# Chunked delta-rule attention with a phase mixer: accumulating products and a tile's transposes issued as several operations each, under a new order, new banks and new engine choices

## The chip, the cores and the metric

The kernel runs on one core of one Trainium2 chip. The metric is the time of one execution in microseconds on the device. Five engines work from queues of their own, each in the order written: TensorE (PE, with its weight loads as PEld), VectorE (DVE), ScalarE (ACT), GpSimd (POOL) and SyncE (SP), which issues most DMA transfers. Inputs and output are float32 in HBM; products run in bfloat16.

## The reference

Four batches of eight heads with 768 steps and 40 channels per head go through a recurrence with a state of 40 x 40 per head. Its output, as 768 x 320 per batch, goes through a mixer with rotated phases.

```python
for t in range(S):
    y[:, :, t] = einsum('bhd,bhde->bhe', rt, state)
    Sa = einsum('bhde,bhe->bhd', state, at)
    state = state * wt[:, :, None, :] - einsum('bhd,bhe->bhde', Sa, bt) \
            + einsum('bhd,bhe->bhde', vt, kt)
# x: (B, S, H*D)
theta = x @ w_theta
zr, zi = x * cos(theta), x * sin(theta)
y = einsum('ts,bsd->btd', w_tok_r, zr) + einsum('ts,bsd->btd', w_tok_i, zi)
u = x + y
out = u + maximum(u @ w_ch, 0)
```

## The kernel before

**Tiles.** A tile is 128 steps of one batch with all heads, 128 x 320. There are 24, six for each batch, numbered i. For each, `prep` takes the logarithm of w (`ln`), sums it along time with a triangular product (`cs`), takes exponentials (`exp` and others) and scales k, b and a with them. Features of 64 rows per head (40 and padding) are turned with PE transposes into `feat`. For tiles 0 to 5 (`TURNED`) raw k, b and a are instead loaded in another layout, two tiles at a time, cast by POOL into `turning` (a view of a z buffer, so the profile shows it as z; `ck`, `cb`, `ca`), turned by PE while still unscaled (`tkbr` for k and b, `tar` for a), and scaled by DVE on the way out of PSUM (`mk`, `mb`, `ma`, L625 and L628). Their exponentials sit in single buffers, `exi` and `exw`.

**Scores and recurrence.** `scores` (L668) makes four products per tile of 128 x 128 per head: psi, phi and the two halves of lam. Each is masked to a triangle on the way from PSUM to SBUF: by DVE with a mask (L676), or by ACT as a plain copy (L678) and then POOL's select (L680). `recurrence` makes x0 = psi v + a state (L712 and L707 in one accumulation), nx, then nu with phi, and the new state gt from k v and b nu (L745). `readout` makes y from the state (L836) and both halves of lam (L842); DVE's `ex` product gives x.

**Mixer.** `theta` turns x for two tiles (`xt`), `sines` multiplies by w_theta and takes cosine and sine on ACT, and z = x cos, x sin is made by POOL or DVE (`product`, L493 and L492). `mix_row` makes a row of the token mixing from twelve products of 320 columns (L896), the largest part of PE's work; it can begin only when the six tiles of a batch are through the recurrence. `channels` then does the product with w_ch and stores. The weights come by POOL's own DMA issues, which also convert to bfloat16: w_theta and w_ch by L935, blocks of w_tok into `wrow` by L946. A copy within SBUF on POOL or ACT (`ws0`, `ws1`) repeats parts of w_theta and w_ch in a second place, since later products read them on other rows.

**Order.** Every step is first recorded as an operation (`Op`) by `Plan.add`, with its engine and with what it reads and writes. `ORDER` lists the numbers of all operations; each engine executes its own in that order. `HOMES` gives the PSUM banks, in the order in which operations open them. `PICK` lists the operations that take their other form, on another engine or as whole transposes (`turn_whole`, 128 x 128, L424) instead of two of 64 rows (`turn`, L419). `WARM` puts idle products (L994) ahead of some operations. An operation is indivisible in this order:

```python
out = [self.ops[n] for n in ORDER]
```

Ahead of the first operation each engine prepares masks and zeroed pads; on POOL the last of this is `sign_col` (L389).

Of the kernel before, what the change touches and what calls it, by code (L numbers as in the profile page):

```python
# [20 lines left out]
LATE = 12  # L21
ORDER = [
# [218 lines left out]
def mm(n):  # L241
    return max(n / 2.4 + 2.5, 25.0)
# [7 lines left out]
def kernel(  # L250
# [252 lines left out]
    def prep(i):  # L503
# [12 lines left out]
        def cs():  # L516
# [7 lines left out]
            if late:  # L524
                return
# [517 lines left out]
```

## Time and profile before

| What | Value |
|---|---|
| Median of 3 runs | 194.38 us (193.88 to 195.51) |
| Span of the profiled execution | 191.6 us |
| Timed runs above the span | 2.3 to 3.9 us, at the median 2.8 |
| Own time of the profiled execution | not recorded apart from its span |
| PE, DVE busy | 179.6, 165.7 us |
| ACT, POOL busy | 157.9, 136.9 us |
| Mean granted TensorE clock | 0.991 |

The span runs from the first to the last instruction on the core. Busy time of PE is a union of overlapping products, so a busy PE need not be at its peak. Rows of a group give the line, engine, operation, tiles and shape, then the busy time in us, the mean duration of one in ns, and after the second bar the idle time of the engine just ahead of them with what ended it. Tile names leave the buffer number out.

### The profile page before, as it was taken

How to read it: one execution, taken by the hardware profiler on the slowest of the kernel's cores; microseconds unless marked ns; L12 is line 12 of the kernel's file. 1: busy time of each engine (PE TensorE's matmuls, PEld its weight loads, DVE VectorE, ACT ScalarE, POOL GpSimd, SP SyncE). 2: the span in 40 equal slices, each digit the busy share in tenths (PEclk: the TensorE clock that was granted, in tenths of full speed). 3: DMA queues.
4: the chain of work that ended last, by engine and by line, in shares of the span. 5: the costliest groups of instructions: out<-in, count | busy, mean ns of one | idle time of the engine just before them, and what ended most of it. 6: DMA issues, size and time to landing. Idle time of an engine off the chain costs nothing.

```text
span 191.6 us, 9477 instructions
## 1 busy us (share of the span) xinstructions
PE 179.6 (94%) x4223; PEld 142.0 (74%) x4223; DVE 165.7 (86%) x268; ACT 157.9 (82%) x288; POOL 136.9 (71%) x162
## 2 busy tenths in 40 slices
PE   7679799999898999999999999999999999999992
PEld 7567587787687877788777787868877877876751
DVE  7599899998899998999889978998999998886552
ACT  3499999999999999989999979799999769883010
POOL 5584595496799789989989396694999983643200
PEclk9969999999999999999999999999999999999999
DMA  5999799989889999999997999999927011001131
GB/s 131 321 310 323 182 244 205 178 150 160 164 137 211 187 187 174 201 215 193 197 207 171 154 191 210 179 169 238 217 38 168 12 37 38 3 3 68 68 140 68
DMA packets 110312, 30.90 MB, mean 161 GB/s; under 512 B 98624, under 2 KB 110272, under 8 KB 110272
## 3 DMA queue, kind: packets, MB, share of 16 engines
q1 hardware_dynamic: 107840, 27.53, 66.6%
q0 software_dynamic: 2432, 2.77, 9.1%
q8 instruction: 33, 0.54, 1.1%
q14 instruction: 7, 0.06, 0.1%
HBM read 29.13 MB, written 3.93 MB: 173 GB/s over the span
## 4 chain that ended last, share of the span: by engine, by line
PE 74%; DVE 13%; ACT 7%; DMA 2%; issue 1%; SPq 1%; POOL 0%; ACTq 0%
PE ps L896 22%; PE ps L419 12%; PE ps L668 10%; PE ps L810 6%; DVE lam L676 4%; PE ps L842 4%; PE ps L424 3%; DMA raw_a<-in_a_dram 2%; PE ps L745 2%; PE ps L816 2%; PE ps L724 2%; PE ps L712 2%; PE ps L836 2%; PE ps L707 2%; PE ps L518 2%; DVE feat L625 2%
## 5 line engine op out<-in xcount | busy, mean ns | idle before, releaser
L676 DVE TENSOR_TENSOR lam<-ps,mask_p 128x1024 bf16<-128x1024 f32 x39 | 47.1, 1219 | 3.6 <-PE ps L668 3.3
L896 PE MATMUL ps<-z,wtok 128*128 128x320 bf16 x288 | 48.2, 299 | 0.0
L493 POOL TENSOR_TENSOR z<-cs,xp 128x640 bf16<-128x640 f32 x21 | 29.2, 1403 | 4.5 <-ACT cs L874 4.4
L896 PEld LDWEIGHTS <-wtok 128*128 128x128 bf16 x288 | 24.3, 97 | 9.1 <-issue 0.2
L493 POOL TENSOR_TENSOR kb<-raw_kb,ex 128x640 bf16<-128x640 f32 x18 | 25.8, 1433 | 2.0 <-ACT nx L718 1.3
L676 DVE TENSOR_TENSOR psi<-ps,mask_p 128x1024 bf16<-128x1024 f32 x19 | 23.1, 1219 | 1.1 <-PE ps L668 1.0
L668 PEld LDWEIGHTS <-feat 64*128 64x128 bf16 x576 | 18.0, 95 | 6.6 <-issue 4.4
L668 PE MATMUL ps<-feat 64*128 64x128 bf16 x384 | 18.4, 221 | 1.9 <-ACT exi L611 0.9
L676 DVE TENSOR_TENSOR phi<-ps,mask_n 128x1024 bf16<-128x1024 f32 x13 | 15.9, 1220 | 1.6 <-PE ps L668 1.6
L680 POOL TENSOR_SCALAR_AFFINE_SELECT phi<-phi 128x1024 bf16<-128x1024 bf16 x11 | 12.0, 1092 | 7.0 <-ACT phi L678 7.0
L842 PE MATMUL ps<-kb,lam 128*128 128x40 bf16 x384 | 15.5, 180 | 0.2 <-DVE lam L676 0.2
L452 ACT COPY feat<-ps 128x1024 f32<-128x1024 f32 (+1 forms) x14 | 14.0, 998 | 0.6 <-PE ps L419 0.5
L842 PEld LDWEIGHTS <-lam 128*128 128x128 bf16 x384 | 13.8, 96 | 0.8 <-issue 0.3
L642 ACT COPY rT<-ps 128x512 bf16<-128x512 bf16 x24 | 13.3, 600 | 0.3 <-PE ps L419 0.2
L509 ACT ACTIVATE lw<-raw_w 128x320 bf16<-128x320 f32 x24 | 11.4, 483 | 2.4 <-DMA raw_w<-in_w_dram 2.3
L680 POOL TENSOR_SCALAR_AFFINE_SELECT lam<-lam 128x1024 bf16<-128x1024 bf16 x9 | 9.8, 1090 | 4.9 <-ACT lam L678 4.9
L901 DVE TENSOR_TENSOR up<-ps,xp 128x320 bf16<-128x320 f32 x22 | 10.6, 487 | 2.8 <-PE ps L896 2.5
L493 POOL TENSOR_TENSOR ah<-raw_a,ex 128x320 bf16<-128x320 f32 x15 | 12.1, 806 | 0.7 <-ACT ex L544 0.4
L452 ACT COPY uT<-ps 128x320 f32<-128x320 f32 (+1 forms) x9 | 3.6, 404 | 10.8 <-PE ps L419 5.4
L678 ACT ACTIVATE phi<-ps 128x1024 bf16<-128x1024 f32 x11 | 11.4, 1033 | 1.0 <-PE ps L668 1.0
L836 PE MATMUL ps<-gd,rT 128*128 128x80 bf16 x80 | 12.2, 197 | 0.0
L728 ACT ACTIVATE nu<-ps 128x320 bf16<-128x320 f32 x24 | 10.8, 450 | 1.5 <-PE ps L724 1.2
(165 smaller groups left out, 538.4 us busy)
## 6 DMA issues: line engine op xcount, KB each, us to landing
raw_w<-in_w_dram SPq DMA_DIRECT2D x24, 160.0 KB, 4.7
raw_r<-in_r_dram SPq DMA_DIRECT2D x12, 320.0 KB, 5.0
out_dram<-oo SPq DMA_DIRECT2D x11, 320.0 KB, 3.1
raw_a<-in_a_dram SPq DMA_DIRECT2D x18, 160.0 KB, 4.5
raw_kb<-in_k_dram SPq DMA_DIRECT2D x18, 160.0 KB, 4.2
raw_kb<-in_b_dram SPq DMA_DIRECT2D x18, 160.0 KB, 4.4
raw_v<-in_v_dram SPq DMA_DIRECT2D x16, 160.0 KB, 5.0
raw_v<-in_v_dram SPq DMA_DIRECT2D x4, 320.0 KB, 5.7
```

What stands on the lines that cost most here:

```text
L419: nc.tensor.transpose(out=dst[:, c, n * 64:n * 64 + 64], in_=block[rows(c)], identity=ident[rows(c), rows(c)])
L452: nc.scalar.copy(out=to, in_=source)
L493: pool = ("POOL", lambda: nc.gpsimd.tensor_tensor(out=dst, in0=in0, in1=in1, op=ALU.mult))
L509: add("ACT", "ln", i, lambda: nc.scalar.activation(out=heads(lw)[:, :, 0:D], in_=raw_w[s4], func=AF.Ln), 473, [("raw_w", s4)], [("lw", s2) ...
L642: add("ACT", "e" + nm, i + x, lambda x=x, dst=dst: nc.scalar.copy(out=dst.rearrange("p g (t q) -> p g t q", q=8), in_=ps(pr).bitcast(BF16) ...
L668: nc.tensor.matmul(t[:, q, g, :], lhsT=lhs[rows(q), g, :], rhs=rhs[rows(q), g, :], start=True, stop=True)
L676: add("DVE", kindm, i, lambda: nc.vector.tensor_tensor(out=flat, in0=whole(), in1=mask.to_broadcast([128, 2 * G, 128]), op=ALU.mult), 1217 ...
L680: add(None, "sel", i, None, 0, dkeys, dkeys, alts=(("POOL", lambda: nc.gpsimd.affine_select(out=flat, in_=flat, pattern=[[0, 2 * G], [1, 1 ...
L810: nc.tensor.matmul(ps(pk)[:, c, 0:DM], lhsT=lhs[:, 3 * c + kt, :], rhs=wt[:, 3 * c + kt, :], start=kt == 0, stop=False, skip_group_check=True)
L836: nc.tensor.matmul(t[:, g * 80:g * 80 + 80], lhsT=rT[:, g, :], rhs=gd[:, 2 * g:2 * g + 2, :], start=True, stop=False, skip_group_check=True)
L842: nc.tensor.matmul(t[:, h * D:h * D + D], lhsT=lam[:, n, p, g, :], rhs=kb[:, n, h, 0:D], start=first and n == 0, stop=n == 1, skip_group_c ...
L896: nc.tensor.matmul(ps(pk)[:, 0:DM], lhsT=wtok[t % NCH][:, c, s, :], rhs=z[:, c, s], start=s == 0 and c == 0, stop=s == NT - 1 and c == 1)
```

## The change

Operations are split where they add into one bank:

- `x0` becomes `x0` (psi v) and `x0s` (the carried state); `y` becomes `yv`, `ys` (state) and `y`; `gt` becomes `gtk` (k v) and `gt` (b nu).
- `cs` loses its last product to `csx`, for tiles before 12.
- The transposes of a tile's features, `tt`, become `tta` (k and b), `ttb` (a) and `ttc` (v), each waiting for its own source alone.

Within a bank the products now mark only the first of them as one that begins the sum. `ORDER` grows from 1390 to 1520 numbers, `PICK` from 134 to 165; `HOMES` has as many entries, with other values. `WARM` places the idle products of the start ahead of other operations, in equal numbers. `TURNED` stays at six tiles. A path for `SIDES` is new, but that set is empty.

Core of the diff:

```diff
+SIDES = frozenset()
 ORDER = [
-    0, 3, 13, 14, 15, 16, 4, 21, 17, 5, 18, 19, 6, 20, 23, 22, 25, 59, 62, 26, 24, 64, 67, 63,
...
+    168, 52, 54, 0, 3, 17, 4, 18, 13, 14, 15, 22, 20, 5, 6, 1, 19, 21, 23, 24, 16, 26, 27, 60,
...
-WARM = {14: (38, 0), 19: (10, 3), 20: (2, 3), 62: (4, 3)}
+WARM = {14: (38, 0), 20: (10, 4), 21: (2, 6), 64: (4, 0)}
...
+        if groups:
+            m = 0
+            for c, (count, keys) in enumerate(groups):
+                add("PE", kind + "abc"[c], i, lambda m=m, count=count: turn(
+                    ps(p).bitcast(BF16), blocks[m:m + count], m), reads=keys, writes=[p],
+                    at=at, new=(p, 2) if c == 0 else None, **quad_cost(4 * count))
+                m += count
...
+        add("PE", "cs", i, cs, mm(328) + 4 * 25, [("lw", s2)], [pk],
+            new=(pk, 1 if late else 2), tail=tail(2))
+        if not late:
+            add("PE", "csx", i, earlier, mm(328), [("lw", s2)], [pk], tail=tail(328))
...
         def x0():
             t = ps(pk)
+            for h in range(H):
+                nc.tensor.matmul(t[:, h * D:h * D + D], lhsT=psi[:, h % 2, h // 2, :],
+                                 rhs=vb[:, h, 0:D], start=h == 0, stop=True,
+                                 skip_group_check=True)
+
+        def carried():
+            t = ps(pk)
             for g in range(G):
...
+                nc.tensor.matmul(t[:, g * 80:g * 80 + 80], lhsT=feat[:, 8 + g, :],
+                                 rhs=gt_old[:, g, :, 0:D], start=False, stop=True,
+                                 skip_group_check=True)
+        add("PE", "x0", i, x0, 8 * 25, [("psi", i % NSC), ("v", i % NRV)], [pk], new=(pk, 1),
+            tail=tail(40))
+        if not first:
+            add("PE", "x0s", i, carried, 4 * mm(80), [("fa", st), ("gt", (i + 1) % 2)], [pk],
+                tail=tail(80))
...
+            add("PE", "gtk", i, lambda: gains(kb[:, 0], vb, True),
+                4 * mm(80) + (mm(320) if join else 0), [("kb", i % NKB), ("v", i % NRV)] +
                 ([("gt", (i + 1) % 2)] if join else []), [gk], new=(gk, 1), tail=tail(80))
+            add("PE", "gt", i, lambda: gains(kb[:, 1], nu, False), 4 * mm(80),
+                [("kb", i % NKB), ("nu", s2)], [gk], tail=tail(80))
...
+        add("PE", "yv", i, lambda: y(0), 8 * 25, [("lam", s2, 0), ("kb", i % NKB)], [pk],
+            new=(pk, 1), tail=tail(40))
+        if not first:
+            add("PE", "ys", i, carried, 4 * mm(80), [("rT", i % 6), ("gd", (i + 1) % 2)], [pk],
+                tail=tail(80))
+        add("PE", "y", i, lambda: y(1), 8 * 25, [("lam", s2, 1), ("kb", i % NKB)], [pk],
+            tail=tail(40))
```

What it moves shows best in the engines' own orders. **POOL at the start**, from the end of its preparation. In these rows raw_kb and raw_a are the loads of k, b and a for tiles 0 and 1, z the buffer that `turning` looks into, and wth the weights of w_theta. Before:

```order
L389 AFFINE_SELECT sign_col_197<-sign_col_197 64x1 x2
L499 CAST z_1_190<-raw_kb_0_71 128x16x40
L499 CAST z_1_190<-raw_kb_1_72 128x16x40
L499 CAST z_1_190<-raw_a_0_68 128x16x40
L499 CAST o_0_130<-raw_v_0_75 128x16x40
L935 DMA wth_233<-in_moe_w_theta_dram 64x320
L499 CAST r_0_132<-raw_r_0_78 128x16x40
```

Now:

```order
L401 AFFINE_SELECT sign_col_197<-sign_col_197 64x1 x2
L991 DMA wrow_1_208<-in_moe_w_tok_r_dram 128x768
L980 DMA wth_233<-in_moe_w_theta_dram 128x2x320
L521 COPY wth_233<-wth_233 64x640
L521 CAST z_1_190<-raw_kb_0_71 128x16x40
L521 CAST z_1_190<-raw_kb_1_72 128x16x40
L521 CAST z_1_190<-raw_a_0_68 128x16x40
L521 CAST r_0_132<-raw_r_0_78 128x16x40
```

Two DMA issues and the copy that repeats a part of wth have moved ahead of the casts; the copy reads what the second of these DMAs writes.

**PE at x0 of tile 10**, with its neighbours (psi and v of that tile, gt the state carried in; products of 320 columns are token mixing, or the sums of a later tile's ln w). Before, the state's products stood between those with psi:

```order
L896 MATMUL ps_0_235<-z_0_189,wtok_0_201 128x320
L707 LDWEIGHTS feat_1_151
L707 MATMUL ps_1_236<-gt_1_137,feat_1_151 128x80
L712 LDWEIGHTS psi_0_158
L712 MATMUL ps_1_236<-v_2_140,psi_0_158 128x40
```

Now:

```order
L730 MATMUL ps_3_238<-v_2_140,psi_0_158 128x40
L941 LDWEIGHTS wtok_1_202
L941 MATMUL ps_1_236<-z_0_189,wtok_1_202 128x320
...
L540 MATMUL ps_1_236<-lw_0_82,ntri_inc_88 128x328
...
L737 LDWEIGHTS feat_1_151
L737 MATMUL ps_3_238<-gt_1_137,feat_1_151 128x80
```

The eight products with psi run first, a piece of the mixing and the sums of another tile stand between, and the four with the state come last into the same bank.

More of the change, by code (lines that the diff above doesn't have):

```diff
@@ L21 @@
 LATE = 12
+SIDES = frozenset()
+SLOT = ((0, 3, 1, 4, 2), (2, 0, 3, 1, 4))
 ORDER = [
[81 rows of a table removed]
-HOMES = [
[13 rows of a table removed]
-PICK = [
[8 rows of a table removed]
-WARM = {14: (38, 0), 19: (10, 3), 20: (2, 3), 62: (4, 3)}
[89 rows of a table added]
+HOMES = [
[13 rows of a table added]
+PICK = [
[10 rows of a table added]
+WARM = {14: (38, 0), 20: (10, 4), 21: (2, 6), 64: (4, 0)}
 class Op:
@@ L414, in pair, with turn @@
         return t[:, 2 * g:2 * g + 2, :].rearrange("p a b -> p (a b)")
-    def turn(dst, blocks):
-        for n, block in enumerate(blocks):
+    def turn(dst, blocks, at=0):
+        for n, block in enumerate(blocks, at):
             for c in range(2):
@@ L427, in quad_cost, with turned @@
         return dict(mode=64, tail=tail(64), cost=n * 8)
-    def turned(kind, kinde, i, blocks, skeys, dst, dkeys, at="tile", eng="ACT", part=64):
+    def turned(kind, kinde, i, blocks, skeys, dst, dkeys, at="tile", eng="ACT", part=64,
+               groups=()):
         p = ("ps", kind, i)
@@ L432, in turned @@
         whole = n <= 8
-        add("PE", kind, i, lambda: turn(ps(p).bitcast(BF16), blocks), reads=skeys, writes=[p],
-            at=at, new=(p, 2), alts=(("PE", lambda: turn_whole(ps(p).bitcast(BF16), blocks)),)
-            if whole else (), **quad_cost(4 * n))
+        if groups:
[5 more added lines that the diff above has]
+                m += count
+        else:
+            add("PE", kind, i, lambda: turn(ps(p).bitcast(BF16), blocks), reads=skeys,
+                writes=[p], at=at, new=(p, 2),
+                alts=(("PE", lambda: turn_whole(ps(p).bitcast(BF16), blocks)),)
+                if whole else (), **quad_cost(4 * n))
         def places(width, source):
@@ L523, in cs, with earlier @@
                                  rhs=ones2, start=False, stop=True, skip_group_check=True)
-            if late:
-                return
+        def earlier():
             before = lw[:, LEAD - 1:LEAD - 1 + H * 64].rearrange("p (h x) -> p h x", x=64)
@@ L528, in cs @@
                              rhs=before[:, :, 0:D + 1], start=True, stop=True)
-        add("PE", "cs", i, cs, (1 if late else 2) * mm(328) + 4 * 25, [("lw", s2)], [pk],
-            new=(pk, 1 if late else 2), tail=tail(2 if late else 328))
+        add("PE", "cs", i, cs, mm(328) + 4 * 25, [("lw", s2)], [pk],
+            new=(pk, 1 if late else 2), tail=tail(2))
+        if not late:
+            add("PE", "csx", i, earlier, mm(328), [("lw", s2)], [pk], tail=tail(328))
         if late:
@@ L566, in prep @@
         blocks = [pair(t, g) for t in (kb[:, 0], kb[:, 1], ah) for g in range(G)]
-        skeys, dkeys = [("kb", i % NKB), ("ah", i % 3)], list(parts)
+        groups, dkeys = [(8, [("kb", i % NKB)]), (4, [("ah", i % 3)])], list(parts)
         if i not in RUNS:
             blocks += [pair(vb, g) for g in range(G)]
-            skeys.append(("v", i % NRV))
+            groups.append((4, [("v", i % NRV)]))
             dkeys.append(("vT", st))
         if i not in TURNED:
-            turned("tt", "et", i, blocks, skeys, feat[:, 0:len(blocks)], dkeys)
+            turned("tt", "et", i, blocks, (), feat[:, 0:len(blocks)], dkeys, groups=groups)
         if i in RUNS and i % 2 == 0:
@@ L704, in x0 @@
             t = ps(pk)
-            for g in range(G):
-                if not first:
-                    nc.tensor.matmul(t[:, g * 80:g * 80 + 80], lhsT=feat[:, 8 + g, :],
-                                     rhs=gt_old[:, g, :, 0:D],
-                                     start=g == 0, stop=False, skip_group_check=True)
-                for p in range(2):
-                    h = 2 * g + p
-                    nc.tensor.matmul(t[:, h * D:h * D + D], lhsT=psi[:, p, g, :],
-                                     rhs=vb[:, h, 0:D], start=first and h == 0,
-                                     stop=True, skip_group_check=True)
-        add("PE", "x0", i, x0, 8 * 25 + (0 if first else 4 * mm(80)),
-            [("fa", st), ("psi", i % NSC), ("v", i % NRV)] +
-            ([] if first else [("gt", (i + 1) % 2)]), [pk], new=(pk, 1), tail=tail(40))
+            for h in range(H):
[4 more added lines that the diff above has]
+            t = ps(pk)
+            for g in range(G):
+                nc.tensor.matmul(t[:, g * 80:g * 80 + 80], lhsT=feat[:, 8 + g, :],
[6 more added lines that the diff above has]
+                tail=tail(80))
         add("ACT", "nx", i, lambda: nc.scalar.copy(out=nx, in_=ps(pk)[:, 0:DM]),
@@ L735, in recurrence, with gains @@
             join = not first and not by_pool
-            def gt_mm():
+            def gains(lt, rt, begin):
                 t = ps(gk)
-                if join:
+                if begin and join:
                     nc.tensor.matmul(t[:, 0:DM], lhsT=ident,
@@ L743, in gt_mm @@
                 for g in range(G):
-                    for j, (lt, rt) in enumerate(((kb[:, 0], vb), (kb[:, 1], nu))):
-                        nc.tensor.matmul(t[:, g * 80:g * 80 + 80], lhsT=pair(lt, g),
-                                         rhs=rt[:, 2 * g:2 * g + 2, 0:D],
-                                         start=not join and j == 0, stop=j == 1,
-                                         skip_group_check=True)
-            add("PE", "gt", i, gt_mm, 8 * mm(80) + (mm(320) if join else 0),
-                [("kb", i % NKB), ("v", i % NRV), ("nu", s2)] +
+                    nc.tensor.matmul(t[:, g * 80:g * 80 + 80], lhsT=pair(lt, g),
+                                     rhs=rt[:, 2 * g:2 * g + 2, 0:D],
+                                     start=begin and not join and g == 0, stop=True,
+                                     skip_group_check=True)
+            add("PE", "gtk", i, lambda: gains(kb[:, 0], vb, True),
+                4 * mm(80) + (mm(320) if join else 0), [("kb", i % NKB), ("v", i % NRV)] +
                 ([("gt", (i + 1) % 2)] if join else []), [gk], new=(gk, 1), tail=tail(80))
+            add("PE", "gt", i, lambda: gains(kb[:, 1], nu, False), 4 * mm(80),
+                [("kb", i % NKB), ("nu", s2)], [gk], tail=tail(80))
             wm = ex_t[i % NEX][:, 0, :, D:D + 1]
@@ L773, in recurrence, with blocks_of @@
                nuT_t[i % 2], [("nuT", i % 2)])
-    def blocks_of(t):
+    def blocks_of(t, sides=False):
+        if sides:
+            split = t.rearrange("p (c k d) -> p k c d", c=2, d=64)
+            return [split[:, kt] for kt in range(5)]
         return [t[:, m:m + 128] for m in range(0, t.shape[1], 128)]
@@ L797, in mixed, with sides @@
         pk = ("ps", kind, q)
+        if not alone(q) and q in SIDES:
+            def sides():
+                for kt in range(5):
+                    for c in range(2):
+                        nc.tensor.matmul(ps(pk)[:, c, 0:DM], lhsT=lhs[rows(c), kt, :],
+                                         rhs=wt[rows(c), SLOT[c][kt], :], start=kt == 0, stop=kt == 4,
+                                         skip_group_check=True)
+            add("PE", kind, q, sides, 5 * mm(320), [lkey] + wkeys, [pk], at=at, new=(pk, 2),
+                tail=tail(320), mode=64)
+            return
         if alone(q):
@@ L830, in readout, with y, carried @@
         pk = ("ps", "y", i)
-        def y():
+        def y(n):
+            t = ps(pk)
+            for h in range(H):
+                nc.tensor.matmul(t[:, h * D:h * D + D], lhsT=lam[:, n, h % 2, h // 2, :],
+                                 rhs=kb[:, n, h, 0:D], start=n == 0 and h == 0, stop=True,
+                                 skip_group_check=True)
+        def carried():
             t = ps(pk)
             for g in range(G):
-                if not first:
-                    nc.tensor.matmul(t[:, g * 80:g * 80 + 80], lhsT=rT[:, g, :],
-                                     rhs=gd[:, 2 * g:2 * g + 2, :], start=True,
-                                     stop=False, skip_group_check=True)
-                for p in range(2):
-                    h = 2 * g + p
-                    for n in range(2):
-                        nc.tensor.matmul(t[:, h * D:h * D + D], lhsT=lam[:, n, p, g, :],
-                                         rhs=kb[:, n, h, 0:D], start=first and n == 0,
-                                         stop=n == 1, skip_group_check=True)
-        add("PE", "y", i, y, 16 * 25 + (0 if first else 4 * mm(80)),
-            [("rT", i % 6), ("lam", s2, 0), ("lam", s2, 1), ("kb", i % NKB)] +
-            ([] if first else [("gd", (i + 1) % 2)]), [pk], new=(pk, 1), tail=tail(40))
+                nc.tensor.matmul(t[:, g * 80:g * 80 + 80], lhsT=rT[:, g, :],
+                                 rhs=gd[:, 2 * g:2 * g + 2, :], start=False, stop=True,
+                                 skip_group_check=True)
+        add("PE", "yv", i, lambda: y(0), 8 * 25, [("lam", s2, 0), ("kb", i % NKB)], [pk],
[5 more added lines that the diff above has]
+            tail=tail(40))
         x = x_of(i)
@@ L859, in theta @@
         src = xs_t[q % 2] if alone(q) else xp_t[q // 2 % (NX // 2)]
-        blocks = blocks_of(src)
+        blocks = blocks_of(src, q in SIDES)
         turned("xt", "ext", q, blocks, sorted({x_key(q), x_key(i)}),
@@ L909, in channels @@
         group = (q,) if alone(q) else (q, q + 1)
-        blocks = blocks_of(src)
+        blocks = blocks_of(src, q in SIDES)
         turned("ut", "eut", q, blocks, [u_key(t) for t in group],
```

212 rows, old and new, of tables (HOMES, ORDER, PICK) are left out of this document.

## The prediction

> **What bounds the kernel now.** I read the page first, then busy time by stretch, then the chain of waits at the start, since the chain shows which wait ends last where the engines are not full.
>
> ```profile
> span 191.6 us, 9477 instructions
> ...
> PE 179.6 (94%) x4223; PEld 142.0 (74%) x4223; DVE 165.7 (86%) x268; ACT 157.9 (82%) x288; POOL 136.9 (71%) x162
> ...
> PE   7679799999898999999999999999999999999992
> ...
> DVE  7599899998899998999889978998999998886552
> ...
> PEclk9969999999999999999999999999999999999999
> ```
>
> ```profile
> 10.00:60.00 50.00, 45.21 (x1252) 37.48 (x1253) 47.28 (x64) 48.47 (x97) 36.46 (x45) 0.97 0.99 204
> 60.00:70.00 10.00, 9.42 (x283) 7.63 (x282) 9.74 (x13) 9.90 (x17) 8.40 (x9) 1.00 1.07 197
> 70.00:187.80 117.80, 117.36 (x2578) 90.40 (x2571) 101.44 (x150) 95.09 (x170) 86.23 (x90) 1.00 0.66 137
> 187.80:191.60 3.80, 0.33 (x3) 0.00 (x0) 0.85 (x2) 0.00 (x0) 0.00 (x0) 1.00 0.24 86
> ```
>
> The columns of the second view are PE, PEld, DVE, ACT and POOL busy, clock, DMA share and rate. Four stages stand out. From 70 us to 187.8 us TensorE is busy for all but 0.44 us: the token mixing gives it work whenever a tile's own chain has none, so nothing done to other engines there shortens the run. From 10 to 60 us there is no such filler, and DVE (2.7 us idle of 50) and ACT (1.5 us idle) set the pace; PE has 4.8 us to spare. The last 3.8 us are the final store. Ahead of 10 us everything hangs on one chain, of which these are the long pieces (start, duration, what):
>
> ```profile
> 2.72 4.74 DMA raw_a<-in_a_dram
> ...
> 7.51 0.73 POOL z L499
> ...
> 8.29 0.43 PE ps L419 x16
> ...
> 8.74 0.70 DVE feat L628
> ...
> 9.52 0.69 ACT exw L613
> ...
> 10.70 0.92 ACT phi L678
> ```
>
> The load of a for tiles 0 and 1 lands, POOL casts it, PE turns it, DVE scales it, ACT takes the exponentials of tile 1, and from there DVE and ACT never rest. So a microsecond lost in the first 10 is lost again at 60, and after 60 PE has a fixed amount left to do. **Start, DVE/ACT pace, then PE work** is how I sum.
>
> **The start.** Both orders give POOL the same preparation. The old one then goes to the casts of raw k, b and a; the new one first issues two weight loads and a copy of wth within SBUF that reads what the second of them writes. The copy is ahead of the three casts on an engine that works in order.
>
> ```profile
> 3.14 0.43 POOL L389 TENSOR_SCALAR_AFFINE_SELECT sign_col<-sign_col 64x1 f32<-64x1 f32 x2
> ...
> 5.21 1.53 POOL L499 CAST z<-raw_kb 128x640 bf16<-128x640 f32 x2 [1.64 <-DMA raw_kb<-in_k_dram]
> ...
> 7.51 0.72 POOL L499 CAST z<-raw_a 128x640 bf16<-128x640 f32 x1 [0.77 <-DMA raw_a<-in_a_dram]
> ```
>
> ```profile
> L946 POOL DMA_DIRECT2D wrow<-in_moe_w_tok_r_dram x6: 528/560/592, 21.6 to 91.8; - x6
> ...
> DMA to landing us min/median/max: 3.8/4.9/5.7
> ```
>
> ```profile
> L499 POOL COPY wth<-wth x2: 712/845/978, 37.2 to 45.7; 64x960 bf16<-64x960 bf16 x1, 64x640 bf16<-64x640 bf16 x1
> ...
> DMA to landing us min/median/max: 4.2/5.3/6.3
> ```
>
> POOL's preparation ends at 3.14 + 0.43 = 3.57 us. The issue for wrow takes 0.56, so the one for wth starts at 4.13. POOL's transfers of this size land 3.8 to 6.3 us after the start of their issue (the wrow row gives 3.8/4.9/5.7, the wth row 4.2 to 6.3). I take the median of the wrow row, 4.9, because the DMA engines are as full here as in most of those cases: landing at 9.0. The copy (0.71, the 64x640 form), the two casts (1.53) and the cast of a (0.72) make 3.0: a is cast by 12.0 us, where it was 8.2. **+3.8 us**; with 3.8 to landing +2.7, with 6.3 +5.2. Behind the waiting copy stand all of POOL's casts; behind those PE's first transposes, DVE's first three products, and, through the single buffers of the exponentials, ACT. The weight transfers move 352 KB ahead of SP's loads as well, but the raw tiles land before POOL comes to them, so this adds nothing here. What the delay absorbs is POOL's old waits of 1.64 and 0.77 us, and these are already in the difference, since it is taken at the end of the cast of a.
>
> A rule of the Trainium skill speaks for a smaller price: its page DMA: Bandwidth & Descriptors, section Anatomy of one DMA, gives a software-issued transfer about 2.0 us plus its bytes at 436 GB/s, an estimate of 2.4 us for these 160 KB, a landing at 6.5 and a loss of 1.3; the sum below would then be 194.3. No transfer of POOL in this trace lands in less than 3.8, so the trace does not agree.
>
> **From 10 to 60 us.** Engine choices change in both directions. Three groups carry most of it:
>
> ```profile
> L676 DVE TENSOR_TENSOR psi<-ps,mask_p 128x1024 bf16<-128x1024 f32 x19 | 23.1, 1219 | 1.1 <-PE ps L668 1.0
> ...
> L680 POOL TENSOR_SCALAR_AFFINE_SELECT lam<-lam 128x1024 bf16<-128x1024 bf16 x9 | 9.8, 1090 | 4.9 <-ACT lam L678 4.9
> ...
> L678 ACT ACTIVATE lam<-ps 128x1024 bf16<-128x1024 f32 x9 | 9.2, 1025 | 0.3 <-PE ps L668 0.2
> ...
> L452 ACT COPY feat<-ps 128x1024 f32<-128x1024 f32 (+1 forms) x14 | 14.0, 998 | 0.6 <-PE ps L419 0.5
> ...
> L456 DVE COPY feat<-ps 128x2048 bf16<-128x2048 bf16 (+1 forms) x4 | 4.6, 1156 | 0.1
> ...
> L493 POOL TENSOR_TENSOR z<-cs,xp 128x640 bf16<-128x640 f32 x21 | 29.2, 1403 | 4.5 <-ACT cs L874 4.4
> ...
> L492 DVE TENSOR_TENSOR z<-cs,xp 128x640 bf16<-128x640 f32 x1 | 1.0, 1001 | 0.0
> ```
>
> Eight maskings go from DVE (71 to 63, 8 x 1.22 = -9.8) to ACT (+8 x 1.03 = 8.2) and POOL (+8 x 1.09 = 8.7). Four copies of feat go the other way (ACT -4.0, DVE +4.6), four z products from POOL to DVE (POOL -5.6, DVE +4.0), and some twenty smaller copies and products change sides. Counted over all, DVE gets 0.8 us more, ACT 0.6 more and POOL 5.7 more. None of it is on the path by itself: over the whole run POOL has 55 us idle and DVE 26. What matters is what stands ahead of a milestone. I take the product that finishes tile 6, at 59.3 us: counting the instructions ahead of it in the orders at the mean durations of their groups, DVE has 52.5 us before and 52.4 now, ACT 58.6 and 58.1. So the new order has no less to do by that point and starts 3.8 us late. It can make good only idle time: none of it, or all 2.7 us of DVE. Its finer pieces should remove some of these small waits; I take **-1.0**, nearer to none, since PE's share of these waits is small, as the next rows show.
>
> **The split products.** x0, y, gt, cs and the transposes of a tile become two or three pieces, so that the part whose operands are ready can run while the other is waited for. What that can bring is the idle time ahead of those groups:
>
> ```profile
> L842 PE MATMUL ps<-kb,lam 128*128 128x40 bf16 x384 | 15.5, 180 | 0.2 <-DVE lam L676 0.2
> ...
> L712 PE MATMUL ps<-v,psi 128*128 128x40 bf16 x192 | 10.8, 180 | 0.0
> ...
> L836 PE MATMUL ps<-gd,rT 128*128 128x80 bf16 x80 | 12.2, 197 | 0.0
> ...
> L707 PE MATMUL ps<-gt,feat 128*128 128x80 bf16 x80 | 9.3, 198 | 0.1
> ...
> L745 PE MATMUL ps<-nu,kb 128*128 128x80 bf16 x80 | 8.3, 201 | 0.0
> ```
>
> Together 0.3 us. The old order had already put other work ahead of each. The pieces cost no arithmetic, but their places change how often PE goes between whole-array products and those on 64 rows, from 168 times to 176. The price of one change is read here:
>
> ```profile
> 97.12 0.28 PE L419 MATMUL ps<-ident,nu 64*128 64x64 bf16 x8
> 97.33 0.99 PE L896 MATMUL ps<-z,wtok 128*128 128x320 bf16 x6
> 98.26 0.32 PE L419 MATMUL ps<-ident,xp 64*128 64x64 bf16 x10
> ```
>
> Six products of 320 columns, each lasting 0.30 us by overlap but with 0.137 between starts (the chain has forty of them in 5.50 us), should fill 0.82; the next group starts after 0.93, so a change costs 0.1. Eight more are 0.8 us. Fourteen whole transposes replace 28 half ones: 14 x 0.055 (128 columns at the same rate) less 28 x 0.015 is about 0.3. PE's own work grows by 1.1. Counted the same way, PE has 129.1 us of work left after tile 6's y before and 129.2 now: the growth lies almost wholly ahead of that point, where PE's 4.8 us of idle time cover it. So **+0.1**.
>
> **After 60 us.** The PE idle time left is 0.58 + 0.44 = 1.0 us. All of it could go, or new waits could arise: POOL has eight more selects, and in its fullest stretch two of them ahead of something that DVE needs would put 2 x 1.09 = 2.2 us on the path. I take **-0.5**.
>
> **The sum.** 3.8 - 1.0 + 0.1 - 0.5 = +2.4, a span of 194.0 us. The timed runs lie 2.8 us above the span at their median (194.4 against 191.6), so **196.8 us**. From the bounds: 2.7 - 2.7 + 0.1 - 1.0 = -0.9 gives 193.5, and 5.2 + 0 + 0.1 + 2.2 = +7.5 gives 201.9.
>
> **Rivals.**
>
> The start is absorbed (A). The transfer lands after 3.8 us, and the new order removes nearly all of DVE's waits up to 60 us: 2.7 - 2.2 + 0.1 - 0.5 = +0.1, so 194.5, with 193 to 195.5 around it. For it: the new order does finish things earlier that lead to the mixing; ahead of the first sines ACT has 1.6 us less and DVE 3.0 less. Against it: it has the same amount ahead of tile 6, and all DVE idle time would have to vanish. The rule of the page cited above would end here too.
>
> Faster (B). The copy does not hold POOL, because the transfer has landed when raw k has, at about 5.2 us; then the pieces remove 2.7 us of DVE waits and 1.0 of PE idle time: -3.6, so 190.8. It decides if the first cast of raw k starts before 6 us. Against it: the issue for wth starts at 4.13, and even the shortest time to landing in the rows leads to 7.9.
>
> Cold start (C). PE now has nothing to do from about 6 to 11 us, and the granted clock, which already fell in the old run, may stay low longer:
>
> ```profile
> 10.00:12.00 2.00, 1.19 (x38) 1.14 (x40) 1.78 (x4) 1.97 (x4) 1.42 (x3) 0.75 1.12 300
> 12.00:15.00 3.00, 2.97 (x65) 2.20 (x60) 3.00 (x4) 2.88 (x7) 2.17 (x3) 0.60 1.15 312
> 15.00:20.00 5.00, 4.75 (x134) 3.95 (x131) 4.95 (x7) 4.99 (x13) 2.11 (x3) 1.00 1.05 291
> ```
>
> Columns as above, the clock being third from the end. If the 4.75 us of PE work that followed at full clock ran at 0.6 to 0.7 of it, it would take some 2.4 us more, and DVE and ACT have no idle time there to hide it: 199.2. Against it: a slow PE at 12 to 15 us left DVE fully busy. The skill's page TensorE: Matmul & The Clock Gate, section on the HAM clock gate, states a fall to half clock after about 3.4 us of idleness and as long a busy time before it rises; the 0.60 here fits a mean of the two, and by that rule the low stretch comes later but is hardly longer.
>
> **How the numbers follow.** Forecast 0.52 (195.5 to 198.5 on its own), A 0.24, B 0.11, C 0.13. About 1% (1.9 us) is what a measurement of this kernel can tell from no change: faster is below 192.4, slower above 196.3. Faster: B and a little of A, 0.12. Within 1%: the rest of A and about a fifth of the forecast, 0.34. Slower: 0.54. The range for 8 in 10 leaves out most of B and the far end of C: 192.8 to 200.2.
>
> **What would show it.** Right: in the new trace POOL's copy of wth is the first thing after its preparation and waits about 4 us on its transfer; the first cast of raw k starts near 9.8 us instead of 5.2, the first scaling of a near 12.5 instead of 8.7; DVE's work is shifted by some 3 us still at 60; PE busy from there on with no more idle time than now. Wrong: a first cast before 7 us, or DVE idle time of under 1 us from 12 to 60, or PE idle time of several us after 70, which would mean that the new order brings waits I have not found.

## The result, and the profile after

| | Before | After |
|---|---|---|
| Median of the runs compared | 194.13 us (193.03 to 195.51) | 213.58 us (212.32 to 214.14) |
| Span of the profiled execution | 191.6 us | 210.6 us |
| Its own time | not recorded apart | 212.32 us |

The ratio is 1.097, interval 1.089 to 1.104: the change costs 19.4 us, where 2.4 were forecast. The medians and ratios here and below leave out executions that took over 1.5% longer than the fastest of the same kernel, one of them 862.74 us. The page of the changed kernel:

```profile
span 210.6 us, 9457 instructions
...
PE 185.7 (88%) x4209; PEld 145.1 (69%) x4209; DVE 166.3 (79%) x274; ACT 158.7 (75%) x283; POOL 142.5 (68%) x169
...
PE   7267988899869979999919999999999998999992
...
DVE  7039899998939978998825969898889979887653
...
POOL 7096048709299794899088899888898886766000
PEclk9858899999979999999975999999999999999999
```

The operations' own work has grown little (DVE +0.6 us busy, ACT +0.8, POOL +5.6; PE +6.1, part of it at a slower clock), so most of the 19 us are waiting. The mean granted clock of this execution is 0.951, where it was 0.991. In its trace the clock is at 0.50 for 20 us (9.0 to 15.9, 19.3 to 22.7, 60.2 to 63.7 and 108.0 to 114.9 us), in that of the kernel before for 3.4. The rows of slices, 5.3 us each, tell where to look: POOL reads 0 in the 2nd slice, 2 in the 11th and 0 in the 20th (5, 53 and 100 us), and each time PE, DVE or the clock is low there or one or two slices later. (Its other zeros, at 21 and 42 us, do not show in PE's row.) The busy time by stretch, columns as before:

```profile
10.00:60.00 50.00, 41.29 (x1086) 33.87 (x1086) 41.83 (x58) 41.18 (x82) 28.45 (x36) 0.91 0.96 205
60.00:70.00 10.00, 9.93 (x230) 8.01 (x229) 7.80 (x10) 8.73 (x14) 9.64 (x13) 0.83 0.99 176
70.00:206.80 136.80, 128.63 (x2846) 98.04 (x2845) 111.62 (x165) 105.21 (x183) 100.41 (x103) 0.98 0.61 122
```

DVE had 2.7 us idle from 10 to 60 and now has 8.2; PE had 0.44 us idle from 70 to the last store and now has 8.2. The view of waits (total, times, longest in us) names what ended them:

```profile
POOL wth L521 <- DMA wth<-in_moe_w_theta_dram: 9.6, 2, 5.8
DVE feat L649 <- PE ps L431: 8.0, 1, 8.0
...
PE ps L751 <- POOL phi L704: 6.8, 2, 4.5
ACT nu L755 <- PE ps L751: 6.7, 3, 4.4
...
POOL wch L521 <- DMA wch<-in_moe_w_ch_dram: 5.8, 1, 5.8
```

The first and the last of these rows are copies within SBUF. The longest wait, DVE's of 8.0 us, lies at the start, behind the first copy. POOL's timeline (start, duration, what, and in brackets the idle time ahead and what ended it) shows the three of them, each behind the issue of the transfer that it reads:

```profile
3.51 0.73 POOL L991 DMA_DIRECT2D wrow<-in_moe_w_tok_r_dram  x1
4.22 0.74 POOL L980 DMA_DIRECT2D wth<-in_moe_w_theta_dram  x1
10.80 0.71 POOL L521 COPY wth<-wth 64x640 bf16<-64x640 bf16 x1 [5.83 <-DMA wth<-in_moe_w_theta_dram]
11.57 1.38 POOL L521 CAST z<-raw_kb 128x640 bf16<-128x640 f32 x2
12.91 0.71 POOL L521 CAST z<-raw_a 128x640 bf16<-128x640 f32 x1
...
53.11 0.57 POOL L980 DMA_DIRECT2D wth<-in_moe_w_theta_dram  x1
57.49 0.98 POOL L521 COPY wth<-wth 64x960 bf16<-64x960 bf16 x1 [3.81 <-DMA wth<-in_moe_w_theta_dram]
...
98.29 0.72 POOL L980 DMA_DIRECT2D wch<-in_moe_w_ch_dram  x1
98.99 0.58 POOL L991 DMA_DIRECT2D wrow<-in_moe_w_tok_i_dram  x1
99.55 0.55 POOL L980 DMA_DIRECT2D wch<-in_moe_w_ch_dram  x1
105.92 0.98 POOL L521 COPY wch<-wch 64x960 bf16<-64x960 bf16 x1 [5.83 <-DMA wch<-in_moe_w_ch_dram]
106.99 1.43 POOL L515 TENSOR_TENSOR kb<-raw_kb,ex 128x640 bf16<-128x640 f32 x1
108.38 1.09 POOL L704 TENSOR_SCALAR_AFFINE_SELECT phi<-phi 128x1024 bf16<-128x1024 bf16 x1
```

POOL stands still for 5.83, 3.81 and 5.83 us. At the third place the next things in its queue are a product for a later tile and the select of phi, which PE's nu needs. PE's timeline there:

```profile
109.52 0.45 PE L751 MATMUL ps<-nx,phi 128*128 128x40 bf16 x8 [4.46 <-POOL phi L704]
```

The chain of waits has two of the three transfers among its longest pieces (start, duration, what):

```profile
53.11 4.26 DMA wth<-in_moe_w_theta_dram
99.55 6.23 DMA wch<-in_moe_w_ch_dram
```

The kernel before has the same copies and the same transfers, but far apart, and one of the two copies of wch runs on ACT there. For wth the prediction showed the copies at 37.2 and 45.7 us; the issues were at 9.7 and 27.3. For wch the view of the tile in the kernel before has

```profile
L935 POOL DMA_DIRECT2D wch<-in_moe_w_ch_dram x2: 570/666/762, 76.9 to 80.1; - x2
L498 ACT COPY wch<-wch x1: 991/991/991, 88.3 to 88.3; 64x960 bf16<-64x960 bf16 x1
L499 POOL COPY wch<-wch x1: 717/717/717, 91.1 to 91.1; 64x640 bf16<-64x640 bf16 x1
```

that is 8 us or more between the issue and the copy, and nothing waits.

How the delay builds up is read from the end of DVE's `ex` product of a tile (its x is then finished), in us. The last two columns are experiments told below:

| Tile | Before | After | Difference | All three copies moved | Start moved too |
|---|---|---|---|---|---|
| 0 | 27.0 | 33.1 | +6.1 | 30.9 | 26.6 |
| 4 | 49.4 | 54.9 | +5.5 | 52.3 | 48.7 |
| 5 | 54.6 | 64.0 | +9.4 | 57.8 | 54.2 |
| 11 | 94.5 | 105.3 | +10.8 | 98.7 | 95.8 |
| 12 | 106.4 | 122.3 | +15.9 | 108.8 | 105.9 |
| 15 | 123.9 | 141.1 | +17.2 | 128.0 | 125.4 |
| 23 | 172.7 | 191.9 | +19.2 | 178.5 | 176.3 |

It jumps at the three places, by 6.1, 3.9 and 5.1 us, and changes less between the first two and between the second and the third. From tile 12 to tile 23 it grows by another 3.3 us. With all three copies moved it grows there by 3.4 and with the start moved too by 4.1, so this part is not the copies': it goes with the rest of the new order, and what in it is open. (So late in the run, the end of a tile also shifts with the mixing work that an order puts ahead of it.)

### The profile page after: what moved, and what is told of

Its sections match the earlier page's. It is cut to its first block, busy times and chain, and to the rows that moved or that the text cites. A ratio compares the mean times of both kernels' runs of the same rounds, so it can differ in the third digit from the quotient of the medians.

```text
span 210.6 us, 9457 instructions
## 1 busy us (share of the span) xinstructions
PE 185.7 (88%) x4209; PEld 145.1 (69%) x4209; DVE 166.3 (79%) x274; ACT 158.7 (75%) x283; POOL 142.5 (68%) x169
## 3 DMA queue, kind: packets, MB, share of 16 engines
q1 hardware_dynamic: 107840, 27.53, 61.4%
q0 software_dynamic: 2432, 2.77, 8.8%
HBM read 29.13 MB, written 3.93 MB: 157 GB/s over the span
## 4 chain that ended last, share of the span: by engine, by line
PE 55%; POOL 14%; ACT 13%; DMA 7%; issue 6%; DVE 3%; POOLq 0%; DVEq 0%; ACTq 0%
PE ps L941 16%; PE ps L431 10%; PE ps L692 7%; PE ps L851 5%; PE ps L876 4%; DMA wch<-in_moe_w_ch_dram 3%; POOL kb L515 3%; DMA wth<-in_moe_w_theta_dram 2%; DMA raw_w<-in_w_dram 2%; PE ps L751 2%; PE ps L436 2%; PE ps L771 2%; POOL phi L704 2%; PE ps L857 2%; PE ps L730 2%
## 5 line engine op out<-in xcount | busy, mean ns | idle before, releaser
L700 DVE TENSOR_TENSOR lam<-ps,mask_p 128x1024 bf16<-128x1024 f32 x33 | 40.0, 1218 | 4.7 <-PE ps L692 4.4
L515 POOL TENSOR_TENSOR z<-cs,xp 128x640 bf16<-128x640 f32 x18 | 25.2, 1412 | 2.0 <-ACT cs L919 2.0
L704 POOL TENSOR_SCALAR_AFFINE_SELECT lam<-lam 128x1024 bf16<-128x1024 bf16 x15 | 17.4, 1162 | 11.5 <-ACT lam L702 11.5
L700 DVE TENSOR_TENSOR psi<-ps,mask_p 128x1024 bf16<-128x1024 f32 x17 | 20.7, 1220 | 1.8 <-PE ps L692 1.4
L876 PE MATMUL ps<-kb,lam 128*128 128x40 bf16 x384 | 17.2, 181 | 0.0
L702 ACT ACTIVATE lam<-ps 128x1024 bf16<-128x1024 f32 x15 | 15.4, 1025 | 0.5 <-PE ps L692 0.5
L515 POOL TENSOR_TENSOR ah<-raw_a,ex 128x320 bf16<-128x320 f32 x17 | 13.7, 807 | 2.8 <-ACT ex L564 1.6
L751 PE MATMUL ps<-nx,phi 128*128 128x40 bf16 x192 | 8.8, 181 | 6.8 <-POOL phi L704 6.8
L649 DVE TENSOR_TENSOR feat<-ps,exi 128x512 bf16<-128x512 bf16 x12 | 7.8, 681 | 8.0 <-PE ps L431 8.0
L751 PEld LDWEIGHTS <-phi 128*128 128x128 bf16 x192 | 7.1, 96 | 8.3 <-POOL phi L704 7.1
```

The lines of the kernel that those rows point to most:

```text
L515: pool = ("POOL", lambda: nc.gpsimd.tensor_tensor(out=dst, in0=in0, in1=in1, op=ALU.mult))
L700: add("DVE", kindm, i, lambda: nc.vector.tensor_tensor(out=flat, in0=whole(), in1=mask.to_broadcast([128, 2 * G, 128]), op=ALU.mult), 1217 ...
L702: 1217, [p], dkeys, alts=(("ACT", lambda: nc.scalar.mul(out=flat, in_=whole(), mul=sign)),))
L704: add(None, "sel", i, None, 0, dkeys, dkeys, alts=(("POOL", lambda: nc.gpsimd.affine_select(out=flat, in_=flat, pattern=[[0, 2 * G], [1, 1 ...
L751: nc.tensor.matmul(t[:, h * D:h * D + D], lhsT=phi[:, h % 2, h // 2, :], rhs=nx[:, h * D:h * D + D], start=False, stop=True, skip_group_ch ...
L876: nc.tensor.matmul(t[:, h * D:h * D + D], lhsT=lam[:, n, h % 2, h // 2, :], rhs=kb[:, n, h, 0:D], start=n == 0 and h == 0, stop=True, skip ...
```

## The experiments

Theory W says that the copies behind their own transfers cost nearly all of the 19 us. The rivals: that the split products and the new order of PE cost it, or that early bytes or a cold clock do. Each experiment moves a few numbers in ORDER. In the changed kernel 168 and 52 are the first issues for wrow and wth, 54 and 53, 55 the first copy and the second issue and copy of wth, 56 and 57 the issues for wch. Ratios are against the kernel before on the same chip. Differences in us are between medians, and those of the kernel before lie between 194.1 and 194.7 us on the chips used, so they carry a doubt of about 0.6 us.

**The splitting alone.** The changed kernel's pieces, run in the order of the kernel before, with its banks, choices and idle products.

```diff
 ORDER = [
-    168, 52, 54, 0, 3, 17, 4, ...
+    0, 3, 13, 14, 15, 22, ...    # each old number replaced by its pieces in a row
```

> The changed kernel's pieces, each set put at the place that the whole operation had in the old order, with the old banks, engine choices and idle products. If splitting costs nothing by itself: 193 to 195.5 us. If pieces cost (more waits, other accumulation): over 198.

Measured: 194.76 us, ratio 1.001 (0.997 to 1.005). The pieces cost and bring nothing by themselves.

**The first three steps alone.** The kernel before with its same three operations (159 wrow, 51 wth, 53 the copy) put at the head.

```diff
 ORDER = [
-    0, 3, 13, 14, 15, 16, ...
+    159, 51, 53, 0, 3, 13, 14, 15, 16, ...
```

> The kernel before with the changed kernel's first three POOL steps alone (wrow issue, wth issue, copy of wth ahead of the first casts). Waits as the cause: 199 to 201 us. If DVE and ACT have enough slack to absorb a late start: 194 to 196.

Measured: 201.51 us, ratio 1.035 (1.030 to 1.039), so 6.7 us from three operations. Its POOL and clock:

```profile
12.05 0.71 POOL L504 COPY wth<-wth 64x640 bf16<-64x640 bf16 x1 [7.09 <-DMA wth<-in_moe_w_theta_dram]
```

```profile
12.00:15.00 3.00, 1.35 (x34) 1.03 (x34) 0.01 (x1) 0.00 (x0) 2.89 (x5) 0.50 1.12 327
15.00:20.00 5.00, 4.28 (x82) 3.45 (x81) 4.50 (x7) 3.04 (x5) 2.83 (x5) 0.50 1.11 321
20.00:25.00 5.00, 4.80 (x85) 3.49 (x84) 4.43 (x5) 4.40 (x11) 3.32 (x6) 0.50 0.71 153
```

In the trace tile 0 ends 8.2 us late, tile 6 7.5 and tile 23 8.2: what is lost at the start is not made good. The clock reads 0.50 up to 25 us.

**Its two issues without the copy.** As the last, with 159 and 51 alone at the head.

> The kernel before with the two DMA issues alone at POOL's start, the copy left where it was. If the early bytes delay SP's loads by themselves: raw w of tile 1 lands some 3 us later (10.9 instead of 8.1) and the time is 196.5 to 199 us. If the loads have slack: 194 to 195.5, and the 6.4 us of the run with the copy come from the copy alone.

Measured: 196.97 us, ratio 1.013 (1.008 to 1.019). Nothing waits for the weights here, and still 2.6 us go: loads land later, that of a at 9.2 us instead of 7.5 and that of w for tile 1 at 11.1 instead of 8.1.

```profile
5.54 1.51 POOL L504 CAST z<-raw_kb 128x640 bf16<-128x640 f32 x2 [0.58 <-DMA raw_kb<-in_k_dram]
9.24 0.72 POOL L504 CAST z<-raw_a 128x640 bf16<-128x640 f32 x1 [2.20 <-DMA raw_a<-in_a_dram]
```

The cast of a starts at 9.24 instead of 7.51, and the clock is at 0.50 from 12 to 20 us. So the 352 KB are not free, and of the 6.7 us of the three steps the copy's wait makes 4.1, by difference. (352 KB is what lands, in bfloat16. Each page shows 29.13 MB read from HBM; SP's loads are 23.6 of these, its 27.53 MB less 3.93 written, and the other 5.53 are twice the 2.77 that POOL's transfers land.)

**Each wait taken away alone** from the changed kernel. First, the copy 54 moved far behind its transfer:

```diff
-    168, 52, 54, 0, 3, 17, ...
+    168, 52, 0, 3, 17, ...
...
-    ... 105, 186, 247, ...
+    ... 105, 186, 54, 247, ...
```

> The changed kernel with the first copy of wth alone moved later, to POOL's place behind a select at about 30 us. Waits as the cause: 207 to 209 us (5 to 6 us less than the change), first cast of raw k at about 5.5 us. If the start is absorbed later: 212 to 214.

Measured: 206.48 us, ratio 1.061 (1.053 to 1.069), 7.1 us less than the changed kernel, a little more than expected. In its trace, of an execution of 209.64 us, the first cast of raw k starts at 5.82 us, that of a at 8.18, yet tile 0 still ends 4.1 us late: the load of w for tile 1 is 3 us late and the clock reads 0.50 from 12.5 us on. The trace with all copies moved, below, has the same at tile 0.

Second, the second issue for wth (53) moved ahead, in its trace to 38.7 us, 17 us before its copy at 55.6:

```diff
-    ... 516, 53, 55, 365, ...
+    ... 516, 55, 365, ...
...
-    ... 189, 105, 186, ...
+    ... 189, 105, 53, 186, ...
```

> The changed kernel with the issue for the second part of wth alone moved ahead by some 15 POOL steps, so that the second copy finds its data landed. If POOL's 3.8 us there are on the path: 209 to 211 us. If other work covers them: 213 to 214.

Measured: 209.38 us, ratio 1.078 (1.071 to 1.084), 4.2 us less, although this execution started later (tile 4 is 7.8 us late). From tile 4 to tile 5 the delay grows by 0.4 us instead of 3.9. Third, both issues for wch moved ahead:

```diff
-    ... 843, 335, 56, 391, 57, 59, 876, ...
+    ... 843, 335, 391, 59, 876, ...
...
-    ... 625, 663, 603, ...
+    ... 625, 663, 56, 57, 603, ...
```

> The changed kernel with the two issues for wch alone moved ahead by some 20 POOL steps, so that the third copy finds its data landed. If POOL's 5.8 us there are on the path, through the select of phi that PE waits 4.5 us for: 207 to 209 us. If other work covers them: 213 to 214.

Measured: 203.3 and 203.8 us, two more runs 208.2 and 209.0, so the times put the gain anywhere between 4.6 and 10.3 us, and no ratio is given. The trace (span 202.1) is closer: it ends 8.5 us ahead of the changed kernel's, but 1.7 of these are there at tile 11, ahead of the copies of wch, which leaves about 7 us for this place. From tile 11 to tile 12 the delay falls by 1.8 us, where it grew by 5.1.

**All three together.**

> The changed kernel with four numbers moved in its order: the first copy of wth behind a later select, and the DMA issues for the second part of wth and for both parts of wch some 20 POOL steps earlier, so that no copy stands right behind the transfer it reads. If the waits of POOL behind those transfers are the cause (5.8 us at the start, 3.8 at 54 us, 5.8 at 100 us in its profile): 195 to 199 us. If the pieces and the new order cost by themselves, or the clock is the cause, over 207 us.

Measured: 198.67 us, ratio 1.023 (1.014 to 1.032): 14.9 of the 19.4 us are gone. The three single effects add up to some 18 us (7.1, 4.2 and about 7), so they overlap in part; where, no run shows. The same kernel was run once more for a trace:

> The changed kernel with all three copies moved away from their transfers, as in the run before, for a trace of it. Theory W (POOL held by copies behind their transfers): no wait of POOL of more than 1 us on wth or wch; the time between 198 and 201 us, span near 197; from 60 us on no PE stop of over 1.5 us that ends on POOL; what is left against the kernel before is the start, 3 to 5 us at the x of tile 0, with the clock at half until about 20 us, since the two weight loads still go ahead of the loads of tile 1. Rival R (a wait of another kind comes in the place of the copies): PE or DVE idle of over 2 us at one place after 70 us, ended by something else.

198.84 us, span 197.1. No wait of POOL on wth or wch is left, and no other long one has come in their place: after 60 us no stop of PE of over 0.6 us ends on POOL, and DVE is never idle for over 1.3 us. The start is as forecast: tile 0 is 3.9 us late, the clock reads 0.50 from 12 to 20 us, and ACT waits 3.79 us for the load of w of tile 1:

```profile
ACT lw L537 <- DMA raw_w<-in_w_dram: 5.2, 2, 3.8
```

**The start repaired too.** As the last, and the first issues for wrow and wth moved behind the casts of the first four tiles.

```diff
-    168, 52, 0, 3, 17, ...
+    0, 3, 17, ...
...
-    ... 149, 114, 116, ...
+    ... 149, 114, 168, 52, 116, ...
```

> The changed kernel with the second and third transfers issued earlier as in the run with four numbers moved, and now the first two DMA issues and the copy behind them also later, past the casts of tiles 0 to 3. If the rest of that run's loss (4.7 us over the kernel before) was the 352 KB ahead of SP's loads and the half clock after the idle start: 193 to 196 us. If it was the new order: 198 to 200.

Measured: 196.88 us, ratio 1.013 (1.007 to 1.019), between the two expectations and 0.9 us above the one for the start alone. 16.7 of the 19.4 us are now gone with five DMA issues and a copy moved, and no product touched. All the rest of the change, the order of the products, the banks and the engine choices, has 2.6 us to account for. Up to tile 7 this kernel is level with the one before or ahead by up to 0.8 us. But by tile 11 it is 1.3 behind and ends 3.6 behind at tile 23. DVE and ACT are as full as before from 10 to 60 us; then comes a stretch in which PE, DVE and ACT each lose some 0.9 to 1.2 us against the kernel before:

```profile
10.00:60.00 50.00, 45.46 (x1243) 37.29 (x1239) 47.59 (x66) 48.27 (x95) 37.18 (x47) 1.00 1.01 204
60.00:70.00 10.00, 8.55 (x254) 6.90 (x254) 8.82 (x11) 8.70 (x17) 8.38 (x10) 1.00 1.08 206
```

In it PE stops without a wait, in the middle of four equal products (the "issue" in brackets is time in which it waited for nothing that the profile shows):

```profile
64.28 0.19 PE L550 MATMUL ps<-ones,lw 128*128 128x2 bf16 x2
65.63 0.20 PE L550 MATMUL ps<-ones,lw 128*128 128x2 bf16 x2 [1.17 <-issue]
```

**What that stop is.** Theory F: PE has run out of instructions. The 24 short transposes of a block of w_tok that stand just ahead were moved later, behind the theta products of tile 2, and with them ACT's copy of their result. In the traces they start at 63.31 us in the repaired kernel and at 68.99 here.

```diff
-    ... 592, 559, 593, 220, 613, 612, ... 575, 221, 659, ... 400, 401, 287, ...
+    ... 592, 559, 593, 613, 612, ... 575, 659, ... 400, 401, 220, 221, 287, ...
```

> The changed kernel with copies and start repaired, and in it the 24 short transposes of one block of w_tok, which stand just ahead of a tile's cs, moved 2.5 us later, behind the theta products of tile 2. In the repaired kernel PE stops 1.17 us in the middle of the four 2-column products of that cs, with no wait shown, just as a packet of instructions arrives. Theory F (PE runs out of instructions after a run of short ones, when the DMA engines are full): 48 fewer instructions ahead take about 0.5 us off PE's use of code, so the stop there shrinks to 0.3 to 0.8 us or goes; the time 196.0 to 196.9, within 0.5% of the repaired kernel's 196.88. Rival M (the stop belongs to the 2-column products themselves, or to the change of row mode ahead of them): it stays at 1.0 to 1.3 us in the same product, the time unchanged at 196.9. Neither: a stop of another size elsewhere shows that it follows the loads.

Measured: 199.02 us, ratio 1.024 (1.019 to 1.030). The time misses both expectations; the stop at that place is gone, as F has it, and there is one elsewhere:

```profile
57.14 0.34 PE L882 MATMUL ps<-kb,lam 128*128 128x40 bf16 x7 [0.94 <-issue]
...
66.30 0.24 PE L550 MATMUL ps<-ones,lw 128*128 128x2 bf16 x4
```

Of the 2.4 us by which its span is longer, 1.3 are there at tile 0, ahead of the edit: in this profile the clock read 0.50 from 12 to 17.5 us, in the repaired kernel's 1.00 throughout, with the same order up to there. The rest comes between tiles 5 and 8, around the new stop at 57 us and some waits of 0.2 to 1.2 us up to 73 us. The new stop is ahead of the edit in PE's stream, where the repaired kernel, with the same instructions, did not stop. So removing the stop by moving work gained nothing.

## Why the prediction was wrong

**The step that failed: the list of what the change does to POOL.** The prediction found one copy behind its own transfer and priced it. The order has three, by the same pattern, and the other two, at 53 and 98 us, were not in the sum. "After 60 us, -0.5" was the term that should have held the third (about 7 us), and the second belonged to the stretch where -1.0 was forecast. Moving their issues alone gives back 4.2 and about 7 us; together that is more than the whole upper end of the sum, +7.5. Bounds drawn around the terms that were found could not hold a term that was not. The reasoning that PE "has a fixed amount left to do" after 60 us, and that "nothing done to other engines there shortens the run", is no bound for the other side: a stopped POOL lengthens it, because a select of phi stands behind the copy and PE's queue is in order too. The sign of failure that the prediction named, several us of PE idle time after 70, is what the profile shows (8.2 us).

**The start: right in mechanism, too small.** The copy is the first thing after POOL's preparation and waits on its transfer. The transfer took 6.5 us from its issue to landing where 4.9 was taken and 6.3 was the upper bound; the copy begins at 10.80 instead of 9.0, the cast of a ends at 13.6 instead of 12.0, a loss of 5.4 instead of 3.8. The Trainium skill's fit (DMA: Bandwidth & Descriptors, section Anatomy of one DMA), an estimate of 2.4 us for these bytes, is further off: 6.5 here, 7.8 in the kernel before with the three steps at its head.

**"This adds nothing here": wrong.** The 352 KB ahead of the loads cost 2.6 us by themselves. The raw tiles of k and b were nearly in time (k landed 0.3 us later), but a landed 1.7 us and the w of tile 1 3.0 us later. The three steps alone cost 6.7 us, where +3.8 was the term and +5.2 its bound.

**The cold start: real, but not the alternative that C made of it.** It came on top of the delay that was forecast. The prediction set C's chance to 0.13 because a short low stretch had left DVE busy; here the low stretch is not short. In the changed kernel it is 10 us in two pieces between 9 and 23 us, where it was 3.4; 3.4 us more follow on the second wait and 6.8 on the third. In the kernel with the three steps at its head it lasts from about 9 to 26 us, though PE is busy 4.3 of 5 us from 15 on. The Trainium skill (TensorE: Matmul & The Clock Gate, part 1 on the HAM clock gate) puts the rise after one busy window of about 3.4 us; these rows do not show that. Whether the small gaps between the products keep it down, or that 112 of the 198 products from 12 to 25 us are transposes, was not tested. No run separates its price cleanly; the two kernels with the same start and different clocks differ by 1.3 us at tile 0.

**A and B fell** with the landing: the first cast starts at 11.57 us, where B needed under 6 and A a landing by 8.

**The recovery of -1.0: not shown to be the new order's.** The repaired kernel is ahead by up to 0.8 us at tile 6, but 0.4 of these are there at tile 0. And the old order recovers as much: with the three steps at its head it is 8.2 us late at tile 0 and 7.5 at tile 6, with the two issues alone 3.7 and 3.0. **"No arithmetic"** was right: the pieces in the old order cost nothing.

**PE's own growth of 1.1 us "covered": not settled.** In the repaired kernel 2.6 us remain. PE's extra work (1.1 by the prediction's count) and its stops without a wait (2.9 us in four places, against 1.3 in the kernel before) are of that size together, but the kernel with the old order has 3.6 us of such stops and ties with the one before. What of the 2.6 us is order, clock or code stays open.

## What to carry to other kernels

When an engine that works in order also issues transfers, go through its whole queue for each operation that reads what an issue shortly ahead of it brings, and not only through the first place that shows it: the distance from issue to use must exceed the time to landing as the loaded DMA engines give it (4.3 to 7.8 us for the transfers that a copy stood behind here), and the price is what stands behind in that queue. A transfer that nobody waits for still costs, if it goes ahead of loads that somebody waits for. A trace of the kernel before cannot show a wait that its own order avoids, so a sum of the terms found can be far too low until every operation that reads a transfer has been gone through.

## What the runs showed of the hardware

PE's stops without a wait lie on a grid in its instruction stream. In six traces (before, after, the old order, all copies moved, the repaired kernel, the moved transposes) the view names 21 stops of 0.3 us or more after 20 us that no releaser ended. Counted in order from 0 over matmuls and weight loads, the instruction behind each stop has a number that is 193 more than a multiple of 256 (705, 1217, 1985, 2241, 2497, 3009, 3265, 4033, 6593), and each stop ends 1.2 to 1.7 us after a packet of the queue for instructions has arrived. The repaired kernel's view of DMA queues (packets, MB, share):

```profile
q8 instruction: 33, 0.54, 1.1%
```

33 packets of 16 KB are one for each 256 of PE's 8,430 matmuls and weight loads. In each trace two to five of these 33 boundaries cost 0.3 to 1.3 us and the others less or nothing. In the 3 us ahead of the costly ones the DMA engines are at a share of 0.7 to 1.3. At 126 of the 158 boundaries after 20 us without such a stop (the last one of each trace left out) the packet had landed over 1.75 us before. The stop in the middle of the four products at L550 is number 3009 in the changed kernel (1.33 us), in the one with all copies moved (1.12) and in the repaired one (1.17), and in the three with one wait taken away (0.96 to 1.40). The Trainium skill (Runtime: NRT & Kernel Launch, section Instruction fetch mechanics) states blocks of 256 instructions fetched by a DMA queue of the engine's own, which fits these counts, and calls the crossing mostly hidden; these stops would be the part that is not. It was not tried to thin out the DMA traffic around one of them.
